# Row-tiled fill in the attention waits of batches 1 and up, v of batch 0 in three head groups, AV moved in the score order

## The chip, the cores and the metric

The kernel runs on one core of one Trainium2 chip. The metric is the device time of one execution in microseconds (us). The engines are TensorE (PE in the profile; its weight loads are PEld), VectorE (DVE), ScalarE (ACT), GpSimd (POOL) and SyncE (SP), which only issues DMAs here.

## The reference

Forgetting attention over 8 batches, 8 heads, 576 positions and a head dimension of 64, and behind it a two-layer network with an exact gelu on 4608 tokens (512 to 2048 to 512).

```python
# attention, for each batch and head
scores = scale * q @ k.T
log_f = np.log(np.clip(f, 0.0001, 1.0))
cum = np.cumsum(log_f, axis=-1)
scores = np.where(causal, -1e9, scores + cum[:, None] - cum[None, :])
attn = softmax(scores)
x = attn @ v                    # heads side by side: 4608 x 512
# feed-forward
h = x @ w_in                    # 512 x 2048
out = gelu_exact(h) @ w_out     # 2048 x 512
```

## The kernel before

**Attention.** Heads are taken in four pairs (`HP`, index `i`), head 0 of a pair on partitions 0 to 63 and head 1 on 64 to 127. For each pair the causal scores are made transposed (keys on partitions) in four score tiles (`STILES`, index `t`), each one or two blocks of keys for both heads. `scores(b, i, t)` (L270) multiplies kT by qT with 64 contraction rows for each head (L289), into one of two buffers of `s_psum`, and ScalarE takes the exp into `e` (L299). Since there are two buffers, the matmuls of a score tile wait until the exp of the tile before the last is done. From pair 1 of batch 1 on, the mask is put on by POOL after the exp (L301). The decay is folded into v: `weigh_v` (L253) multiplies v by exp(-cum) on POOL (or DVE) and adds a column of weights, so that the row sum comes out of the same product. AV is `attend` (L313): 15 matmuls for a head (L320), with e as the weights, into an `o_psum` buffer; `normalize` (L328) divides on DVE (L333, L334). `to_xT` or a DMA transpose turns x for the next product.

**Feed-forward.** For each batch `gemm1` (L370) makes 16 blocks of h from w_in (L375), each in an `m_psum` bank that ScalarE empties by the gelu (L392). The second product, with w_out, is not made at once: it is cut into steps, which are generators (`yield` after a step), and taken as fill between the score tiles of the next batch, where TensorE would wait for ScalarE. `take(fill, n)` takes n steps; the tables `FILL` (batches 3 to 7), `FILL_2` (batch 2) and `FILL_1` (batch 1) give n after each score tile, and their last row the number taken before the AV of pair 3.

**Row-tiled steps.** `gemm2_rows` (L446) makes a 128 x 512 output block in 16 steps from a string: "n" is one matmul with 128 contraction rows into the first bank; "r" is two matmuls of 64 rows each, one on each half of the array, into two banks. At the end DVE copies the second bank to SBUF (L474) and adds the first (L476). `PLAN` gives, for batches 3 to 7, four blocks: which pool holds the two banks ("o", "m", "s") and the string. Batch 0's second product is split in two halves of `n_ff`: `gemm2_half` (L485) uses 128-row steps (L501) for two output blocks, half 0 in the waits of batch 1, half 1 at the head of batch 2's fill (`gemm2_third`), where `PLAN_0` and `PLAN_1` follow.

**PSUM.** There are eight banks: two buffers of two banks in `s_psum`, two of one in `o_psum` (tag "o"), two of one in `m_psum` (tag "m"). A new tile takes a buffer of its pool when its former tile has been read.

**Order.** The schedule is written by hand: every engine does its instructions in the order of the program text. In batches 3 to 7 (`attention`, L621) each pair is score tile 0, fill, tile 1, fill, AV of the pair before, tile 2, fill, tile 3, fill. Batch 0 (`first_attention`, L527) and batch 1 (`second_attention`, L656) have orders of their own. SP's queue issues the loads of v (`load_v`, L114: five DMAs, one for each block of keys, of 256-byte rows), POOL's queue those of q, k, w_in and w_out. `gate` (L562) makes POOL wait for a part of v before it issues w_in; `weigh_v` of later head pairs, the loads of v, w_in, q and k for batch 1 stand behind it on POOL and SP.

Of the kernel before, what the change touches and what calls it, by code (L numbers as in the profile page):

```python
# [52 lines left out]
def kernel(  # L53
# [78 lines left out]
    load_v(0, 0, 4)  # L132
# [261 lines left out]
    def gemm2(c):  # L394
# [38 lines left out]
        (1, "m", 5 * "r" + "n" + 9 * "r" + "n"),  # L433
        (2, "m", 9 * "r" + "n" + 6 * "r"),
# [11 lines left out]
    def gemm2_rows(c, plan):  # L446
# [4 lines left out]
        for ts, held, steps in plan:  # L451
# [10 lines left out]
            for kt, step in enumerate(steps):  # L462
                last = kt == steps.rindex("r")
                for r in range(2 if step == "r" else 1):
# [5 lines left out]
                        start=(kt == 0),  # L470
# [14 lines left out]
    def gemm2_half(c, half):  # L485

        pss = [
            m_psum.tile([P, d_model], FP32, tag="m", name="ps2") for _ in range(2)
        ]
        k0, k1 = half * n_ff // 2, (half + 1) * n_ff // 2  # L490
        if half:
            order = [(ts, kt) for ts in range(2) for kt in range(k0, k1)]
        else:
            order = [
                (ts, kq + kt)
                for kq in (0, 4)
                for ts in range(2)
                for kt in range(4)
            ]
        for ts, kt in order:  # L500
            nc.tensor.matmul(  # L501
                pss[ts],
                g_of[c][kt][:, ts * P : (ts + 1) * P],
                w_out_sb[:, kt, :],
                start=(kt == k0),
                stop=(kt == k1 - 1),
            )
            if kt == k1 - 1 and not half:
                ot_of.append(o_pool.tile([P, d_model], FP32, tag="ot", name="ot"))
                (nc.scalar.copy if ts else nc.vector.tensor_copy)(ot_of[ts], pss[ts])  # L510
            elif kt == k1 - 1:
                nc.vector.tensor_tensor(ot_of[ts], ot_of[ts], pss[ts], Alu.add)
                store(c, ts, ot_of[ts])
            yield
# [12 lines left out]
    def first_attention():  # L527
# [28 lines left out]
        transposes(2, m_psum, "m")  # L556
        scores(0, 1, 1)
# [3 lines left out]
        weigh_v(0, 0, nc.vector)  # L561
        gate = x_pool.tile([P, 1], FP32, tag="gate", name="gate")  # L562
        nc.gpsimd.tensor_copy(gate[D:P], v_sb[D:P, 0, 4, 0:1])
# [11 lines left out]
        load_qk_tokens(1, 4, 8)  # L575
        scores(0, 2, 0)
        scores(0, 2, 1)
        scores(0, 2, 2)
        scores(0, 2, 3)
        attend_head(0, 0)  # L580
        scores(0, 3, 0)
        attend_head(0, 1)
        scores(0, 3, 1)
        attend_head(1, 0)
        scores(0, 3, 2)
        attend_head(1, 1)
        scores(0, 3, 3)
        to_xT(0, 0, nc.vector.tensor_copy)
        attend_head(2, 0)
# [66 lines left out]
    def second_attention():  # L656
# [16 lines left out]
        for i in range(HP):  # L673
            for t in range(4):
# [4 lines left out]
                if i and t in (1, 2):  # L679
                    av(i - 1, t - 1)  # L680
# [81 lines left out]
```

## Time and profile before

| | us |
|---|---|
| median of 8 runs | 349.25 |
| lowest, highest run | 348.09, 350.45 |
| the profiled execution | 349.2 |
| its span, first to last instruction | 347.1 |
| TensorE busy | 331.0 |
| ScalarE busy | 212.6 |
| VectorE busy | 187.6 |
| GpSimd busy | 124.3 |

The granted TensorE clock was 0.998 of full speed. The span falls into batch 0 (until about 40), batch 1 (to 73), batch 2 (to 120), batches 3 to 7 (36.3 each, to 301.5) and the tail with the last products. A line of the timeline is the start, the length of the merged group, engine, line and operation, output and inputs, rows by columns of the TensorE array, shape and type, and the number of instructions; in brackets the idle time of the engine before the group, and what ended it. A line of the chain of waits is start, length, what.

### The profile page before, as it was taken

The numbers are of one execution on the slowest core, as the hardware profiler recorded it, in microseconds if no ns is written. First come the engines' busy times: TensorE is split into PE (matmuls) and PEld (weight loads), VectorE is DVE, ScalarE is ACT, GpSimd is POOL, SyncE is SP. The second block draws the span as 40 slices with busy tenths as digits, with TensorE's granted clock in tenths as the row PEclk, the third lists the DMA queues.
The fourth block names the chain that finished last, engine by engine and source line by source line (L and its number), as shares of the span: only waits on it lengthen the run. The fifth ranks groups of instructions, "written<-read, shape, count | busy, mean of one in ns | idle before, by whom it ended". The sixth has DMA issues, their size and how long they took to land.

```text
span 347.1 us, 7895 instructions
## 1 busy us (share of the span) xinstructions
PE 331.0 (95%) x3182; PEld 175.4 (51%) x3227; DVE 187.6 (54%) x424; ACT 212.6 (61%) x296; POOL 124.3 (36%) x256
## 2 busy tenths in 40 slices
PE   7799999999999999999999999999999999999995
PEld 3574555445554455545654465446544554444443
DVE  5770355943367935796479646975597542021011
ACT  5887786773734787368746973687468765503600
POOL 8390662238318044533445242714270430000000
PEclk9999999999999999999999999999999999999999
DMA  8999999969993999278935995399800130011013
GB/s 119 173 179 195 206 146 169 175 137 160 230 180 94 143 206 178 65 111 163 211 106 75 138 211 136 69 161 205 157 30 2 52 100 30 2 60 60 0 34 90
DMA packets 99924, 43.03 MB, mean 124 GB/s; under 512 B 78704, under 2 KB 95344, under 8 KB 99888
## 3 DMA queue, kind: packets, MB, share of 16 engines
q1 hardware_dynamic: 82592, 28.37, 40.7%
q0 software_dynamic: 16896, 13.63, 26.7%
q8 instruction: 25, 0.41, 0.5%
q10 hardware_dynamic: 400, 0.52, 0.4%
q14 instruction: 11, 0.09, 0.1%
HBM read 36.85 MB, written 9.44 MB: 133 GB/s over the span
## 4 chain that ended last, share of the span: by engine, by line
PE 85%; ACT 6%; issue 3%; POOL 2%; DVE 2%; DMA 2%; POOLq 0%; ACTq 0%; DVEq 0%
PE ps L375 35%; PE ps L466 21%; PE o L320 9%; PE ps L408 8%; PE s L289 7%; ACT e L299 3%; PE ps L501 2%; DMA k<-in_k_dram 2%; ACT L299 2%; PE ps_x L353 1%; ACT g L392 1%; DVE x L334 1%; POOL q L107 1%; PE ps_f L206 1%; POOL k L107 1%
## 5 line engine op out<-in xcount | busy, mean ns | idle before, releaser
L392 ACT ACTIVATE g<-ps 128x512 bf16<-128x512 f32 x144 | 85.3, 597 | 81.1 <-PE ps L375 81.1
L299 ACT ACTIVATE e<-s 128x896 bf16<-128x896 f32 (+2 forms) x128 | 101.5, 836 | 31.9 <-PE s L289 29.2
L375 PE MATMUL ps<-xT,w_in_sb 128*128 128x512 bf16 x497 | 111.4, 379 | 0.8
L466 PE MATMUL ps<-w_out_sb,g 64*128 64x512 bf16 (+1 forms) x731 | 100.5, 376 | 0.8 <-issue 0.8
L375 PEld LDWEIGHTS <-w_in_sb 128*128 128x128 bf16 x576 | 56.0, 98 | 67.5 <-issue 1.8
L301 POOL TENSOR_SCALAR_AFFINE_SELECT e<-e 128x256 bf16<-128x256 bf16 (+1 forms) x135 | 49.3, 383 | 103.3 <-ACT e L299 103.0
L466 PEld LDWEIGHTS <-g 64*128 64x128 bf16 (+1 forms) x756 | 41.5, 94 | 40.9 <-issue 11.9
L289 PE MATMUL s<-qT,kT 64*128 64x320 bf16 (+4 forms) x384 | 45.9, 277 | 4.5 <-ACT e L299 2.7
L244 DVE COPY qT<-tq 64x288 bf16<-64x288 bf16 x96 | 48.7, 507 | 1.4
L260 POOL TENSOR_TENSOR vw<-v_sb,wT 128x640 bf16<-128x640 f32 x31 | 39.7, 1281 | 22.7 <-PE ps L501 12.6
L320 PE MATMUL o<-vw,e 128*128 128x65 bf16 x960 | 36.8, 194 | 3.5 <-issue 2.4
L474 DVE COPY ot<-ps 128x512 f32<-128x512 f32 x26 | 17.9, 690 | 40.3 <-PE ps L466 40.3
L320 PEld LDWEIGHTS <-e 128*128 128x128 bf16 x960 | 34.8, 98 | 5.3 <-PE ps_x L353 0.3
L244 DVE COPY kT<-tk 64x288 bf16<-64x288 bf16 x96 | 32.7, 341 | 1.6
L289 PEld LDWEIGHTS <-kT 64*128 64x128 bf16 x384 | 20.1, 94 | 25.3 <-issue 12.3
L334 DVE TENSOR_TENSOR x<-o,r 128x320 bf16<-128x320 f32 x64 | 31.5, 492 | 2.4 <-DVE r L333 0.2
L417 DVE COPY ot<-ps 128x512 f32<-128x512 f32 (+2 forms) x9 | 5.7, 632 | 48.8 <-PE ps L408 31.9
L408 PE MATMUL ps<-w_out_sb,g 128*128 128x512 bf16 (+2 forms) x142 | 27.9, 355 | 0.1
L333 DVE RECIPROCAL r<-o 128x5 f32<-128x5 f32 x64 | 12.1, 189 | 26.7 <-PE o L320 26.6
L408 PEld LDWEIGHTS <-g 128*128 128x128 bf16 x144 | 13.5, 98 | 14.5
L476 DVE TENSOR_TENSOR ot<-ot,ps 128x512 f32<-128x512 f32 x26 | 17.9, 687 | 1.5
L365 POOL COPY tails<-xT 128x256 bf16<-128x256 bf16 x8 | 3.2, 399 | 31.2 <-DVE xT L356 31.2
(64 smaller groups left out, 158.5 us busy)
## 6 DMA issues: line engine op xcount, KB each, us to landing
out_dram<-ot SPq DMA_DIRECT2D x32, 256.0 KB, 2.3
v_sb<-in_v_dram SPq DMA_DIRECT2D x24, 256.0 KB, 5.2
q<-in_q_dram POOLq DMA_DIRECT2D x6, 576.0 KB, 6.1
k<-in_k_dram POOLq DMA_DIRECT2D x6, 576.0 KB, 8.1
v_sb<-in_v_dram SPq DMA_DIRECT2D x22, 128.0 KB, 5.5
w_in_sb<-in_moe_w_in_dram POOLq DMA_DIRECT2D x4, 512.0 KB, 6.7
w_out_sb<-in_moe_w_out_dram POOLq DMA_DIRECT2D x4, 512.0 KB, 8.3
q<-in_q_dram POOLq DMA_DIRECT2D x4, 144.0 KB, 4.4
```

The costliest lines, as they stand in the source:

```text
L244: nc.vector.tensor_copy(rows[:, odd], src[odd * D : (odd + 1) * D, 2 * i + h].rearrange("d j p -> d p j"),)
L260: eng.tensor_tensor(vw_of[b][:, hs, :, 0:D], v_sb[:, hs, :, :], w.unsqueeze(3).to_broadcast([P, 2, NBLK, D]), Alu.mult,)
L289: nc.tensor.matmul(to, *ab, start=half < 0, stop=half == 1 or not masked)
L299: nc.scalar.activation(et[:, :, z:c], st[:, :, z:c], Act.Exp, scale=scale)
L301: nc.gpsimd.affine_select(out=et[:, :, c0 + z : c0 + P], in_=et[:, :, c0 + z : c0 + P], compare_op=Alu.is_ge, fill=0.0, base=z, pattern=[[ ...
L320: nc.tensor.matmul(o[:, m, :], e_of[b, i, t][:, h, c : c + P], vw_of[b][:, 2 * i + h, n, :], start=(n == 0), stop=(n == m),)
L334: nc.vector.tensor_tensor(x_of[b, i][:, :, h, :], o[:, :, 0:D], r.unsqueeze(2).to_broadcast([P, NBLK, D]), Alu.mult,)
L375: nc.tensor.matmul(ps, w_in_sb[:, kt, ffb * P : (ffb + 1) * P], src[:, kt, 0:TC], start=(kt == 0), stop=(kt == n_dm - 1),)
L392: nc.scalar.activation(g_of[c][ffb], ps, Act.Gelu)
L408: nc.tensor.matmul(pss[ts][:, c0:c1], g_of[c][kt][:, ts * P : (ts + 1) * P], w_out_sb[:, kt, c0:c1], start=(kt == 0), stop=(kt == n_ff - 1),)
L466: nc.tensor.matmul(banks[r], g_of[c][kt][rows, ts * P : (ts + 1) * P], w_out_sb[rows, kt, :], start=(kt == 0), stop=last if r else kt == n ...
L474: nc.vector.tensor_copy(ot, banks[1])
```

## The change

Six edits, all in the order or the form of the work; the arithmetic is the same but for the order of sums.

1. v of batch 0 is loaded in three groups of heads (0-1, 2-3, 4-7) instead of two (0-3, 4-7).
2. The gate waits for a load of the second group (head 2, block 2), over all partitions, instead of the last of the first group.
3. In batch 0, the weighing of v for heads 0 and 1 on DVE moves ahead of the transposes of pair 3, and AV of pair 0 starts before the scores of pair 2, where it stood behind all four of them; the rest follows.
4. `gemm2_half` becomes row-tiled: one output block at a time, two banks, eight steps of two 64-row matmuls, and two DVE operations to empty them; the first block of half 1 uses `o_psum`.
5. In batch 1 the fill starts in pair 1 (`FILL_1`), both AVs of pairs 1 and 2 stand behind tile 1 of the next pair, and one `to_xT` moves.
6. In batches 3 to 7 `FILL` takes one step more behind tiles 0 and 1 of pair 0 (one less behind tile 2), and one step behind tile 0 of the other pairs (one less behind tile 1), seven instead of eight before the AV of pair 3; `PLAN` moves its "n" steps so that each is again the last before an AV, which makes one of them the first step of block 2, and the `start` flag follows.

```diff
--- before.py
+++ after.py
@@ -129,7 +129,8 @@
     make_identity(nc, ident_bf)
     load_qk_tokens(0, 4, 6)
     nc.gpsimd.memset(v_sb[:, :, 0, 0:1], 0.0)
-    load_v(0, 0, 4)
+    load_v(0, 0, 2)
+    load_v(0, 2, 4)
 
 
     key_of = consts.tile([P, 2, P], BF16)
@@ -430,8 +431,8 @@
 
     PLAN = [
         (0, "o", 16 * "r"),
-        (1, "m", 5 * "r" + "n" + 9 * "r" + "n"),
-        (2, "m", 9 * "r" + "n" + 6 * "r"),
+        (1, "m", 6 * "r" + "n" + 9 * "r"),
+        (2, "m", "n" + 9 * "r" + "n" + 5 * "r"),
         (3, "s", 7 * "r" + 9 * "n"),
     ]
 
@@ -467,7 +468,7 @@
                         banks[r],
                         g_of[c][kt][rows, ts * P : (ts + 1) * P],
                         w_out_sb[rows, kt, :],
-                        start=(kt == 0),
+                        start=kt == (steps.index("r") if r else 0),
                         stop=last if r else kt == n_ff - 1,
                     )
                 if kt == n_ff - 1 if held == "s" else last:
@@ -484,34 +485,37 @@
 
     def gemm2_half(c, half):
 
-        pss = [
-            m_psum.tile([P, d_model], FP32, tag="m", name="ps2") for _ in range(2)
-        ]
+
         k0, k1 = half * n_ff // 2, (half + 1) * n_ff // 2
-        if half:
-            order = [(ts, kt) for ts in range(2) for kt in range(k0, k1)]
-        else:
-            order = [
-                (ts, kq + kt)
-                for kq in (0, 4)
-                for ts in range(2)
-                for kt in range(4)
+        for ts in range(2):
+            pool, held = (o_psum, "o") if half and not ts else (m_psum, "m")
+            banks = [
+                pool.tile([P, d_model], FP32, tag=held, name="ps2") for _ in range(2)
             ]
-        for ts, kt in order:
-            nc.tensor.matmul(
-                pss[ts],
-                g_of[c][kt][:, ts * P : (ts + 1) * P],
-                w_out_sb[:, kt, :],
-                start=(kt == k0),
-                stop=(kt == k1 - 1),
-            )
-            if kt == k1 - 1 and not half:
-                ot_of.append(o_pool.tile([P, d_model], FP32, tag="ot", name="ot"))
-                (nc.scalar.copy if ts else nc.vector.tensor_copy)(ot_of[ts], pss[ts])
-            elif kt == k1 - 1:
-                nc.vector.tensor_tensor(ot_of[ts], ot_of[ts], pss[ts], Alu.add)
-                store(c, ts, ot_of[ts])
-            yield
+            for kt in range(k0, k1):
+                for r in range(2):
+                    rows = slice(r * D, (r + 1) * D)
+                    nc.tensor.matmul(
+                        banks[r],
+                        g_of[c][kt][rows, ts * P : (ts + 1) * P],
+                        w_out_sb[rows, kt, :],
+                        start=(kt == k0),
+                        stop=(kt == k1 - 1),
+                    )
+                if kt == k1 - 1:
+                    if not half:
+                        ot_of.append(
+                            o_pool.tile([P, d_model], FP32, tag="ot", name="ot")
+                        )
+                        nc.vector.tensor_copy(ot_of[ts], banks[0])
+                    else:
+                        nc.vector.tensor_tensor(
+                            ot_of[ts], ot_of[ts], banks[0], Alu.add
+                        )
+                    nc.vector.tensor_tensor(ot_of[ts], ot_of[ts], banks[1], Alu.add)
+                    if half:
+                        store(c, ts, ot_of[ts])
+                yield
 
     def gemm2_third():
         yield from gemm2_half(0, 1)
@@ -554,13 +558,13 @@
         nc.vector.tensor_copy(wT[D:P, 4, :], psw[D:P, 4, :])
         scores(0, 1, 0)
         transposes(2, m_psum, "m")
+        weigh_v(0, 0, nc.vector)
         scores(0, 1, 1)
         scores(0, 1, 2)
         transposes(3, m_psum, "m")
         scores(0, 1, 3)
-        weigh_v(0, 0, nc.vector)
         gate = x_pool.tile([P, 1], FP32, tag="gate", name="gate")
-        nc.gpsimd.tensor_copy(gate[D:P], v_sb[D:P, 0, 4, 0:1])
+        nc.gpsimd.tensor_copy(gate, v_sb[:, 2, 2, 0:1])
         load_w_in(0)
         weigh_v(0, 1)
         load_w_in(1)
@@ -573,21 +577,21 @@
         load_w_in(3)
         load_qk_tokens(1, 0, 4)
         load_qk_tokens(1, 4, 8)
+        attend_head(0, 0)
         scores(0, 2, 0)
+        attend_head(0, 1)
         scores(0, 2, 1)
         scores(0, 2, 2)
+        attend_head(1, 0)
         scores(0, 2, 3)
-        attend_head(0, 0)
+        attend_head(1, 1)
         scores(0, 3, 0)
-        attend_head(0, 1)
+        to_xT(0, 0, nc.vector.tensor_copy)
         scores(0, 3, 1)
-        attend_head(1, 0)
+        attend_head(2, 0)
         scores(0, 3, 2)
-        attend_head(1, 1)
+        attend_head(2, 1)
         scores(0, 3, 3)
-        to_xT(0, 0, nc.vector.tensor_copy)
-        attend_head(2, 0)
-        attend_head(2, 1)
         to_xT(0, 1, nc.scalar.copy)
         attend_head(3, 0)
         both = s_psum.tile([P, 2, 1024], BF16, tag="s", name="ps_x2")
@@ -614,9 +618,9 @@
 
 
 
-    FILL = [[6, 5, 4, 3], [0, 4, 3, 3], [0, 4, 3, 3], [0, 4, 3, 3], [8]]
+    FILL = [[7, 6, 3, 3], [1, 3, 3, 3], [1, 3, 3, 3], [1, 3, 3, 3], [7]]
     FILL_2 = [[8, 8, 8, 8], [8, 8, 4, 4], [4, 4, 4, 4], [4, 4, 4, 4], [8]]
-    FILL_1 = [[0, 0, 0, 0], [0, 0, 0, 0], [2, 2, 2, 2], [2, 2, 2, 2]]
+    FILL_1 = [[0, 0, 0, 0], [2, 0, 0, 2], [0, 4, 2, 2], [1, 2, 0, 1]]
 
     def attention(b):
 
@@ -676,10 +680,13 @@
                 if i == 0 and t < 3:
                     transposes(t + 1, *((m_psum, "m") if t == 1 else (o_psum, "o")))
                 take(fill, FILL_1[i][t])
-                if i and t in (1, 2):
-                    av(i - 1, t - 1)
-                if i > 1 and t == 0:
+                if i == 2 and t == 0 or i == 3 and t == 1:
                     to_xT(b, i - 2, nc.vector.tensor_copy, o_psum, "o")
+                if i == 1 and t in (1, 2):
+                    av(0, t - 1)
+                if i > 1 and t == 1:
+                    av(i - 1, 0)
+                    av(i - 1, 1)
                 if (i, t) == (1, 3):
                     load_qk_tokens(2, which="k")
                 if (i, t) == (3, 0):
```

## The prediction

> **What bounds the kernel now.** I read the page's busy times and its chain first, then the timeline of one late batch (the stretch from 228.9 to 265.2 us, which repeats every 36.3 us), then batches 1, 2 and 0.
>
> ```profile
> PE 331.0 (95%) x3182; PEld 175.4 (51%) x3227; DVE 187.6 (54%) x424; ACT 212.6 (61%) x296; POOL 124.3 (36%) x256
> PE 85%; ACT 6%; issue 3%; POOL 2%; DVE 2%; DMA 2%; POOLq 0%; ACTq 0%; DVEq 0%
> ```
>
> TensorE is the bound: 331.0 of 347.1 us, and 85% of the chain. No matmul is removed, so only waits of TensorE and drains between its modes can be gained, about 16 us in all. In the late batch they are these:
>
> ```profile
> 230.56 1.24 PE L466 MATMUL ps<-w_out_sb,g 64*128 64x512 bf16 x10
> 230.92 3.13 ACT L299 ACTIVATE e<-s 128x896 bf16<-128x896 f32 x4
> 231.88 0.37 PE L289 MATMUL s<-qT,kT 64*128 64x448 bf16 x2
> ...
> 237.93 0.74 PE L289 MATMUL s<-qT,kT 64*128 64x256 bf16 x8
> 238.49 0.82 PE L466 MATMUL ps<-w_out_sb,g 64*128 64x512 bf16 x6
> 239.35 0.69 DVE L474 COPY ot<-ps 128x512 f32<-128x512 f32 x1 [2.08 <-PE ps L466]
> 239.47 1.11 PE L320 MATMUL o<-vw,e 128*128 128x65 bf16 x30 [0.16 <-issue]
> 240.15 0.69 DVE L476 TENSOR_TENSOR ot<-ot,ps 128x512 f32<-128x512 f32 x1
> 240.72 0.97 PE L466 MATMUL ps<-w_out_sb,g 64*128 64x512 bf16 x6
> ```
>
> Ends of matmuls are modelled and overlap, so I compare starts. A fill step of two half-row matmuls takes 0.216 us (lower down: 16 of them, 1.73 us in the chain). Ten matmuls from 230.56 are five steps and end at 231.64; the next score tile starts at 231.88, when the first exp (0.92 us from 230.92) is done: 0.24 us of wait. Score tiles 0 and 1 of pair 2 start at 237.93 and their fill at 238.49: 0.56 us where the tiles alone take 0.19 + 0.16, so 0.20 us of wait; the same reading gives 0.18 for pair 1 and about 0.17 for pair 3. The rest of the batch is dense.
>
> **What the skill says.** TensorEngine Tiling (Array Packing), Key Properties: a change of tiling mode drains TensorE. The chain agrees and gives the price:
>
> ```profile
> 73.47 1.83 PE ps L501 x8
> ...
> 77.70 1.73 PE ps L466 x16
> ```
>
> Eight full steps before a row-tiled score tile take 0.10 us more than eight row-tiled ones; the way in costs the same (score tile 73.10, full fill 73.40: 0.30 against 0.19 at 81.12). The same page, Gotcha 1: PSUM Pressure: row tiles write different banks, and evacuation may become the limit. Here each row-tiled output block holds two banks and needs two DVE passes of 0.69 us (L474, L476). TensorE: Matmul & The Clock Gate, Part 3, The mechanism: matmuls are strictly first in, first out. The trace agrees (AV, ready, starts behind the score tile that waits 0.49 us at 45.58), so a fill matmul that waits stops all behind it. DMA: Bandwidth & Descriptors, Anatomy of one DMA: about 2.0 us fixed per transfer, which overlaps; the fastest v load took 2.6 us to land.
>
> **Batches 3 to 7 (FILL, PLAN).** Per batch the gains are: two more steps before tile 2 of pair 0, and one step between tiles 0 and 1 of pairs 1, 2 and 3, with one fewer after tile 1. Going through the batch with the starts above (tile 0 0.19, tile 1 0.16, tile 2 0.20, tile 3 0.14, step 0.216): tile 2 of pair 0 moves from 231.88 to 232.08, tile 1 of pair 1 stays at 234.10 (exp bound), with two more steps done: 0.43 gained. AV of pair 0 starts 0.22 sooner. Tile 1 of pair 2 then starts at 238.11 with the extra step behind it.
>
> Now the step that costs. The steps taken are 7, 13, 16, 19, then 20, 23, 26, 29, then 30, 33: tile 1 of pair 2 takes steps 30, 31 and 32. Steps 30 and 31 end block ts 1, and step 32 is the new leading "n" of block ts 2, whose two banks come from the same two m_psum buffers. It must wait for DVE to empty one. Before, step 32 stood behind AV of pair 1 (1.05 us) and waited little: the six matmuls at 240.72 take 0.97 instead of 0.82, since the first starts (240.72) before the add ends (240.84), the second after it. So the new block's first bank is the one that the copy (L474) releases, the second that of the add. After: the last "r" starts at t, the copy at t + 0.43 (238.92 to 239.35), ends at t + 1.12, and "n" starts at t + 1.17. Unhindered it would start at t + 0.33 (step 0.216, drain 0.11). The stall is 0.84 us, and AV of pair 1, the scores of tiles 2 and 3 and all later exps stand behind it. The old 0.17 at 240.72 goes.
>
> Following on: AV of pair 1 moves from 239.47 to 239.88, tile 1 of pair 3 from 242.68 to 242.96 (exp and TensorE arrive together), AV of pair 2 from 243.82 to 243.89; the last fill before AV of pair 3 has one step fewer, so that AV, and the batch's end, comes 0.15 us sooner. Nothing else there changes its mode switches: every "n" still stands just before an AV. Five batches: -0.75 us.
>
> **Batch 2.** gemm2_half(0, 1) fills two waits with full-row steps: four mode switches of 0.10 to 0.11, all removed: -0.4. Added are two adds of 0.69 on DVE, which here waits for TensorE (3.57 us idle before its first add); the o_psum banks of its first block are empty about 1 us before step 16. The weight loads double, beside the matmuls, as in the other row-tiled fills.
>
> **Batch 1.** TensorE waits for exps:
>
> ```profile
> 45.58 0.34 PE L289 MATMUL s<-qT,kT 64*128 64x64 bf16 x4 [0.49 <-ACT e L299]
> 47.90 0.37 PE L289 MATMUL s<-qT,kT 64*128 64x256 bf16 x4 [0.28 <-ACT e L299]
> 48.20 0.39 PE L501 MATMUL ps<-w_out_sb,g 128*128 128x512 bf16 x1
> ```
>
> Two steps (0.43) fit before 45.58 and two before 47.90, free. Pairs 2 and 3 then have twelve steps instead of sixteen (-0.87) and four mode switches fewer each (about -0.8). But both AVs now stand behind tile 1: in pair 2, tile 1 starts at 48.58 (before 49.02), four steps, a drain and two AVs put tile 2 at 50.75 (before 50.30), and ACT runs dry for about 1.2 us; in pair 3 two steps, to_xT and two AVs put tile 2 at 54.93 (before 54.78). Tile 3's exp ends at 56.90 (before 57.21). The new DVE adds (four passes of 0.69 where there were a copy on DVE and one on ACT) hold the bank of step 8's second row about 0.3 us, and end before xT of pair 2 has to be copied out. So -0.2; bounds -0.9 (AVs hidden better) and +0.5. w_out's first chunk lands at 44.5, and the first fill comes at 44.9 less what batch 0 gains: a tie, in the bounds.
>
> **Batch 0.** The weights and v:
>
> ```profile
> 14.43 0.56 PE L206 MATMUL ps_f<-ident_bf,k 96*64 96x96 bf16 x12 [0.54 <-DMA k<-in_k_dram]
> 16.11 0.20 PE L289 MATMUL s<-qT,kT 64*128 64x64 bf16 x2 [0.43 <-ACT e L299]
> 16.92 0.37 PE L289 MATMUL s<-qT,kT 64*128 64x448 bf16 x2 [0.44 <-ACT e L299]
> 17.62 0.31 PE L289 MATMUL s<-qT,kT 64*128 64x320 bf16 x2 [0.25 <-ACT e L299]
> ```
>
> The wait for k of heads 6 and 7 stays. After it, 1.1 us of waits on exps can hold AV (0.58 a head), if v is weighted by 15.2. Heads 0 and 1 are a quarter of the bytes; the first five v loads land from 10.3 to 15.0, so I put this quarter at 11 to 13, and the weighing on DVE (0.82 us, now ahead of two copies of 0.76) between 13.3 and 14.3. SP issues 15 loads instead of 10 (about 0.5 us each[...]). The gate falls on the eighth load, which may land about 1 us sooner than 14.95, so w_in starts sooner and meets the third v group. POOL's queue behind the gate: w_in, three weighings of 1.3, v of batch 1, q and k; v of heads 4 and 5 is needed at 20.4 instead of 21.9, when it is weighted now by 20.0. Stepping through gives exps ending at 23.1 instead of 22.56, but the AV that follows starts at 23.1 instead of 23.57 (it waited for DVE to free its bank): -0.45. k landing sooner, since less v is queued before it, could give up to 1 us more; a late third group costs up to 0.5. I take -0.7, bounds -1.5 and +0.5.
>
> **Sum.** -0.75 - 0.4 - 0.2 - 0.7 = -2.05 us. The profiled execution took 349.2 (span 347.1), and the median of the runs is 349.25, so the same base serves: 347.2.
>
> **Rivals.**
> *No change* (349.0): batches 0 and 1 give nothing (+0.9), and the stall is 0.2 longer in five batches (+1.0): -0.15 is left. For it: ACT runs dry in batch 1.
> *Slower* (350.9): the leading "n" gets the bank of the add, not of the copy. It then waits 0.74 us more, in five batches +3.7. It decides from a stall of 1.25 us on (0.84 + 2.05/5). Against it: the start at 240.72.
> *Much faster* (343.0): the "n" finds a free bank and doesn't stall: 5 x 0.84 = 4.2 us more. Against it: m_psum has two buffers, and both are held by block ts 1.
>
> **How the numbers follow.** Forecast 0.55 (346.0 to 348.6), no change 0.20, slower 0.17, much faster 0.08. The range 345.2 to 350.0 leaves out the last two in part. This kernel's measurement can't tell less than 0.3% (1.05 us) from nothing: faster is below 348.2. Faster: 0.48 of the forecast and 0.08, 0.56; within: 0.07 and 0.18, 0.25; slower 0.17 and 0.02, 0.19.
>
> **What would show it.** In a late batch: no wait before tile 2 of pair 0, a gap of about 0.8 us before the first AV matmul of pair 1 that ends with L474, a period of 36.15. In batch 2, L501 rows of 64. In batch 1, ACT idle about 1.2 us before tile 2 of pair 2. The prediction is wrong if the gap is absent or 1.5 us, or if batch 0's gemm1 starts later than 25.1.

## The result, and the profile after

| | median, us | lowest to highest | ratio to before |
|---|---|---|---|
| before, 56 runs | 348.93 | 348.05 to 352.75 | |
| changed, 19 runs | 351.92 | 348.70 to 354.29 | 1.006, 95% interval 1.0039 to 1.0081 |

The change makes the kernel 0.6% slower; the forecast was 0.6% faster, and the median lies above its range. The execution profiled with the result is a long one (358.2 us, TensorE clock 0.982, above all 19 runs of the table), so a second profile of the same kernel, called *again* below (353.4 us, span 351.0), stands beside it. In the changed kernel the lines are one higher up to the half product, whose matmul is L498 for L501 (scores L290, AV L321, copy L475).

The page of *again*, busy times and chain by engine:

```profile
PE 330.6 (94%) x3221; PEld 175.4 (50%) x3259; DVE 192.1 (55%) x429; ACT 211.8 (60%) x295; POOL 124.4 (35%) x256
...
PE 81%; DMA 8%; POOL 3%; issue 3%; DVE 2%; SPq 2%; ACT 0%; POOLq 0%; DVEq 0%; ACTq 0%
```

TensorE is as busy as before (331.0), and the span is 3.9 us longer (of the 4.2 us by which this execution is longer than the one profiled before, 0.4 lie outside the span): waits were added, and DMA, 2% of the chain before, is 8% now. Where they lie, the starts of the stages tell (a stage runs to the next one's first matmul; the last stage, the tail, starts with the matmul on the tails of x; worked out from the timelines):

| stage, us | before | again | profile of the result | old v (experiment 3) | edits 1 to 3 alone (experiment 9, second profile) |
|---|---|---|---|---|---|
| batch 0, to its first L376 | 25.10 | 24.29 | 30.29 | 25.08 | 25.64 |
| batch 0, gemm1 | 15.40 | 15.41 | 15.40 | 15.41 | 15.40 |
| batch 1, attention | 18.26 | 22.83 | 18.28 | 18.27 | 18.26 |
| batch 1, gemm1 | 14.34 | 14.35 | 14.34 | 14.34 | 14.34 |
| batch 2, attention | 33.00 | 32.57 | 32.57 | 32.97 | 33.01 |
| batch 2, gemm1 | 13.91 | 14.52 | 17.74 | 13.90 | 13.91 |
| batches 3 to 7 and on, to the tail | 195.20 | 194.52 | 194.55 | 194.53 | 195.21 |
| tail | 31.93 | 32.51 | 32.58 | 31.89 | 32.60 |
| span | 347.14 | 351.00 | 355.75 | 346.39 | 348.37 |

Batches 2 to 7 did what the prediction says (-0.43, and -0.68 in the five late ones). Four rows lose: batch 1 in *again* (+4.57), batch 0 in the profile of the result (+5.19), gemm1 of batch 2 in both (+0.61 and +3.83), and the tail wherever v is loaded in three groups (+0.6).

**Batch 1.** The timeline of TensorE in *again*, leaving out lines between:

```profile
43.91 0.37 PE L290 MATMUL s<-qT,kT 64*128 64x256 bf16 x4
46.24 1.04 PE L498 MATMUL ps<-w_out_sb,g 64*128 64x512 bf16 x4 [1.96 <-DMA w_out_sb<-in_moe_w_out_dram]
47.06 0.53 PE L290 MATMUL s<-qT,kT 64*128 64x64 bf16 x4
...
50.13 1.06 PE L498 MATMUL ps<-w_out_sb,g 64*128 64x512 bf16 x4
```

The first fill step, new behind tile 0 of pair 1, stands for 1.96 us for the first chunk of w_out, issued at 37.9 (before: 37.8) and landed at 46.2 (44.5). Before, its first use was at 48.20. Its four matmuls then last 1.04 where four take 0.60 elsewhere. Windows of *again*, and of before (start and end, length, busy times with counts of PE, PEld, DVE, ACT and POOL, then clock, DMA share and GB/s):

```profile
44.00:46.00 2.00, 0.28 (x4) 0.02 (x3) 0.84 (x2) 1.51 (x2) 0.99 (x4) 0.94 1.13 180
46.00:52.00 6.00, 5.76 (x55) 3.28 (x55) 1.38 (x4) 2.77 (x4) 1.86 (x6) 0.50 0.72 113
```

```profile
44.00:46.00 2.00, 1.51 (x36) 0.96 (x31) 1.64 (x3) 1.84 (x3) 1.37 (x2) 1.00 1.24 209
46.00:52.00 6.00, 5.67 (x87) 3.55 (x86) 2.81 (x9) 5.01 (x7) 3.91 (x10) 1.00 0.86 119
```

From the end of the wait on TensorE has half its clock for 6 us (0.50 against 1.00), and gets through 55 matmuls where it did 87. Old v, experiment 3, has the same batch 1 without the wait: counted from the start of the batch, *again* is 2.1 us behind it at the first fill (46.24) and 4.6 us behind at 54.54, when the clock is full again. So of the 4.57 us 1.96 are the wait, and the remaining 2.6 fall into this stretch.

**Batch 0.** The timeline of POOL and TensorE in the profile of the result:

```profile
14.26 0.79 POOL L170 DMA_DIRECT2D w_in_sb<-in_moe_w_in_dram  x1
...
23.52 1.27 POOL L261 TENSOR_TENSOR vw<-v_sb,wT 128x640 bf16<-128x640 f32 x1 [6.26 <-DMA v_sb<-in_v_dram]
...
25.02 0.98 PE L321 MATMUL o<-vw,e 128*128 128x65 bf16 x15 [5.63 <-POOL vw L267]
```

AV of head 4 stands 5.63 us for v of its head, the new third group (the clock is half for 6.8 us from 22.3 on, within this wait). The last load of that group was issued at 14.83, 0.57 behind w_in's first chunk; its issue in this profile, and the one of *again* (issued at 14.9, w_in 0.4 behind it), with the time to landing at the end of the line:

```profile
v_sb<-in_v_dram SPq DMA_DIRECT2D x1, 64.0 KB, 8.5
```

```profile
v_sb<-in_v_dram SPq DMA_DIRECT2D x1, 64.0 KB, 2.6
```

The -0.81 of *again* in the first row is not a gain of the new order. Four profiles have batch 0 as it was: that of before, that of experiment 2, and the first and the last of experiment 13. There gemm1 starts at 25.10, 24.67, 24.06 and 24.16, by when k of heads 6 and 7 lands (14.38, 13.96, 13.30, 13.67). The first matmul on this k, and gemm1, in the first profile of experiment 13 and in *again*:

```profile
13.42 0.53 PE L206 MATMUL ps_f<-ident_bf,k 96*64 96x96 bf16 x12
...
24.06 0.81 PE L375 MATMUL ps<-xT,w_in_sb 128*128 128x512 bf16 x3
```

```profile
13.51 0.53 PE L207 MATMUL ps_f<-ident_bf,k 96*64 96x96 bf16 x12
...
24.29 0.81 PE L376 MATMUL ps<-xT,w_in_sb 128*128 128x512 bf16 x3
```

From that matmul to gemm1 the four take 10.45 to 10.67 us, and *again* takes 10.78: its batch 0 is shorter than before's since k landed 0.97 us sooner (13.41). Whether three groups of v make k land sooner is not settled (12.85 to 14.37 in 14 profiles, 13.30 to 14.38 in the six with two groups).

**Batches 3 to 7.** The chain of waits in *again*, late batch (start, length, what):

```profile
241.99 0.45 PE ps L467 x4
242.46 0.70 DVE ot L475
243.17 0.04 issue
243.21 0.38 PE ps L467
243.59 0.95 PE o L321 x30
```

The leading n stands for the copy, and AV of pair 1 behind it, as worked out: no fill runs from 242.46 to 243.21. In *again* the timeline gives this wait as 0.78 (predicted 0.84).

### The profile page after: what moved, and what is told of

Same layout as the page of the kernel before. It is cut to its first block, busy times and chain, and to the rows that moved or that the text cites. A ratio compares the mean times of both kernels' runs of the same rounds, so it can differ in the third digit from the quotient of the medians.

```text
span 355.8 us, 7969 instructions
## 1 busy us (share of the span) xinstructions
PE 331.2 (93%) x3221; PEld 175.8 (49%) x3259; DVE 192.2 (54%) x429; ACT 211.4 (59%) x295; POOL 124.2 (35%) x256
## 4 chain that ended last, share of the span: by engine, by line
PE 86%; DMA 3%; issue 3%; DVE 2%; SPq 2%; POOL 2%; ACT 1%; POOLq 0%; ACTq 0%; DVEq 0%
PE ps L376 35%; PE ps L467 24%; PE o L321 9%; PE ps L409 8%; PE s L290 7%; DMA v_sb<-in_v_dram 2%; SPq L119 2%; PE ps L498 2%; PE ps_x L354 1%; DVE ot L475 1%; DMA xT<-x 1%; ACT e L300 1%; POOL q L107 1%; DVE x L335 1%; PE ps_f L207 1%
## 5 line engine op out<-in xcount | busy, mean ns | idle before, releaser
L376 PE MATMUL ps<-xT,w_in_sb 128*128 128x512 bf16 x497 | 113.2, 383 | 2.8 <-DMA xT<-x 2.0
L467 PE MATMUL ps<-w_out_sb,g 64*128 64x512 bf16 (+1 forms) x736 | 104.0, 376 | 4.7 <-DVE ot L475 3.9
L376 PEld LDWEIGHTS <-w_in_sb 128*128 128x128 bf16 x576 | 56.4, 98 | 70.9 <-issue 6.4
L467 PEld LDWEIGHTS <-g 64*128 64x128 bf16 (+1 forms) x756 | 39.9, 94 | 40.5 <-issue 10.6
L245 DVE COPY qT<-tq 64x288 bf16<-64x288 bf16 x96 | 46.8, 487 | 1.4
L321 PE MATMUL o<-vw,e 128*128 128x65 bf16 x960 | 38.0, 196 | 9.0 <-POOL vw L267 5.6
L290 PE MATMUL s<-qT,kT 64*128 64x320 bf16 (+4 forms) x384 | 44.4, 278 | 1.7 <-ACT e L300 0.8
L321 PEld LDWEIGHTS <-e 128*128 128x128 bf16 x960 | 35.5, 99 | 15.2 <-issue 6.6
L475 DVE COPY ot<-ps 128x512 f32<-128x512 f32 x26 | 17.9, 689 | 37.2 <-PE ps L467 37.2
L245 DVE COPY kT<-tk 64x288 bf16<-64x288 bf16 x96 | 36.9, 384 | 1.6
L290 PEld LDWEIGHTS <-kT 64*128 64x128 bf16 x384 | 18.9, 94 | 20.7 <-issue 4.1
```

The source lines that it names most:

```text
L245: nc.vector.tensor_copy(rows[:, odd], src[odd * D : (odd + 1) * D, 2 * i + h].rearrange("d j p -> d p j"),)
L290: nc.tensor.matmul(to, *ab, start=half < 0, stop=half == 1 or not masked)
L321: nc.tensor.matmul(o[:, m, :], e_of[b, i, t][:, h, c : c + P], vw_of[b][:, 2 * i + h, n, :], start=(n == 0), stop=(n == m),)
L376: nc.tensor.matmul(ps, w_in_sb[:, kt, ffb * P : (ffb + 1) * P], src[:, kt, 0:TC], start=(kt == 0), stop=(kt == n_dm - 1),)
L467: nc.tensor.matmul(banks[r], g_of[c][kt][rows, ts * P : (ts + 1) * P], w_out_sb[rows, kt, :], start=kt == (steps.index("r") if r else 0), ...
L475: nc.vector.tensor_copy(ot, banks[1])
```

## Experiments

Expectations of the first eight runs name theories by letters: A, the third group of v comes late since w_in's loads start ahead of it; B, the loss is the leading n's stall; C, a lower clock alone; D, fifteen loads instead of ten are late by SP's issuing; E, batch 1's first fill stands for w_out, and the clock falls behind that. Runs of one group share their runs of before; medians of before were 348.78 (first four), 349.53 (next four), 348.86 and 349.08 (the last two groups of four); the two further profiles in 9 have one run of before, 348.81.

**1. The same kernel again.** No edit.

> The changed kernel once more, for a second profile. Theory A (the third group of v lands late because w_in, released by the earlier gate, runs beside it): the AV of head 4 in batch 0 waits for the weighing of v by 1 to 6 us, varying from run to run, and batch 0's gemm1 starts between 24.5 and 30; time 350 to 353. Theory B (the loss is the leading full-row step of block 2 in batches 3 to 7): that wait is small here and the late batches take over 36.7 us each. Theory C (a lower granted clock or a slow load elsewhere made the profiled run long): no wait over 1 us in batch 0, time near 349.

351.78, ratio 1.0089 (1.0059 to 1.0118). It gave the profile above: the loss repeats, and the clock before the wait in batch 1 is full, so C alone falls. A's wait isn't in this execution: AV of head 4 doesn't wait, AV of head 2 stands 0.73 us for its v. Its six times run from 349.32 to 353.43: waits on DMAs differ from execution to execution.

**2. Tables of batches 3 to 7 alone.**

```diff
# before.py, with the changed PLAN, FILL and start flag only
-    FILL = [[6, 5, 4, 3], [0, 4, 3, 3], [0, 4, 3, 3], [0, 4, 3, 3], [8]]
+    FILL = [[7, 6, 3, 3], [1, 3, 3, 3], [1, 3, 3, 3], [1, 3, 3, 3], [7]]
```

> The kernel before with FILL, PLAN and the start flag of the change alone (batches 3 to 7). My sum gives 0.15 us less in each of five batches: about 348.3, a period of 36.15, with a wait of 0.8 us on L474 ahead of AV of pair 1. Theory B: 352 or more. A bank released by the add would give a wait of 1.5 us and about 352.

348.68, 0.9992 (0.9972 to 1.0011), the period 36.17 instead of 36.29: the small gain, with its stall, is there in the trace, though the time can't be told from before's. B is not the loss.

**3. v in two groups, with the former gate; the rest changed ("old v").**

```diff
-    load_v(0, 0, 2)
-    load_v(0, 2, 4)
+    load_v(0, 0, 4)
...
-        nc.gpsimd.tensor_copy(gate, v_sb[:, 2, 2, 0:1])
+        nc.gpsimd.tensor_copy(gate[D:P], v_sb[D:P, 0, 4, 0:1])
```

> The changed kernel with v in two groups and the gate of the kernel before; order of batch 0 and all fills as changed. Theory A: heads 0 to 3 land near 15.0, so the first AV waits for the weighing until about 16, but no wait over 1 us behind it; gemm1 of batch 0 starts at 24.5 to 25.5, time 347.5 to 349. Theory B: 351 or more.

349.09, 1.001 (0.9997 to 1.0023). This edit alone takes back most of the loss. Batch 0 ends at 25.08: the first AV has to wait for its v, and from the matmul on k it takes 11.2 us; and batch 1 is 18.27: its first fill comes at 44.90, and w_out had landed at 44.77, so it escapes the wait by 0.13 us. A second profile of this very kernel, under the name old_v_no_stall:

> The run with the former loads and gate of v once more, as a look beside the others: the first fill step meets w_out about when it lands (44.8 before), so a wait of 0 to 0.5 us; span 346.4, within 0.5 of it.

350.0, span 347.96: chunk 0 landed at 45.2, the first fill came at 45.4 without a wait. Batch 0 was 0.5 us longer, and AV in batch 2 stood 0.7 us for the mask on POOL: the span expected, 346.4, was missed by 1.6.

**4. The gate behind the last load of the third group.** The weighing of heads 2 and 3 goes ahead of it.

```diff
-        nc.gpsimd.tensor_copy(gate, v_sb[:, 2, 2, 0:1])
+        nc.gpsimd.tensor_copy(gate[D:P], v_sb[D:P, 4, 4, 0:1])
```

> The changed kernel with w_in queued behind the last load of the third group of v (and the weighing of heads 2 and 3 ahead of the gate). Theory A: the third group lands by about 17.5, AV of head 4 waits less than 0.5 us, gemm1 of batch 0 starts near 23.6 instead of 25.1 in the kernel before, and the time is 346 to 348. Theory B: still 351 or more. Theory D (fifteen v loads instead of ten are late by themselves, through SP's issue): AV of head 4 still waits over 2 us, time 350 or more.

353.5, 1.0135 (1.0114 to 1.0157): worse. v lands by 17.6, so D falls, but AV of head 4 still stands:

```profile
21.32 0.63 PE L321 MATMUL o<-vw,e 128*128 128x65 bf16 x15 [1.81 <-POOL vw L267]
```

POOL issues two chunks of w_in from 18.2 on, behind the gate, and weighs v of heads 4 and 5 only then, from 19.8 to 21.3. The clock is half for 3.4 us behind this wait, and batch 0 ends at 26.39. So A's forecast of this run fails as well: v in time is not enough, since the gate also holds the weighing. The first fill of batch 1 stands for w_out here as well. The timeline and the window behind it:

```profile
48.00 0.61 PE L498 MATMUL ps<-w_out_sb,g 64*128 64x512 bf16 x4 [1.62 <-DMA w_out_sb<-in_moe_w_out_dram]
```

```profile
47.00:50.00 3.00, 2.00 (x38) 1.36 (x39) 0.58 (x2) 1.69 (x3) 1.32 (x5) 1.00 1.25 197
```

A wait of 1.62 us, and here the clock stays at 1.00: batch 1's attention is 19.82, only the wait longer. So E's second part isn't tied to every such wait.

**5. The gate on the first group.**

```diff
-        nc.gpsimd.tensor_copy(gate, v_sb[:, 2, 2, 0:1])
+        nc.gpsimd.tensor_copy(gate, v_sb[:, 0, 2, 0:1])
```

> The changed kernel with the gate on a load of the first group of v, so that w_in is issued near 11, ahead of the whole third group. Theory A (a v load issued after w_in lands with it): the last v load lands after 20, AV of head 4 waits 3 to 7 us in every run, time 354 or more. If the late third group in the first profile had another cause: no wait over 1 us there, time near 352 or less.

352.21, 1.01 (1.005 to 1.015). With w_in issued at 11.1, all five loads of the third group land from 18.3 to 21.1, AV of head 4 stands 2.78 us, the clock is half for 3.4 us behind it, and batch 0 ends at 27.84. A's mechanism is there, w_in ahead of v delays v, but the wait and the time are smaller than A expected (3 to 7 us, 354).

**6. w_out ahead of the first weighing of batch 1's v on POOL.**

```diff
                 if ffb == 12:
-                    weigh_v(1, 0)
                     load_w_out(0)
                     load_w_out(1)
+                    weigh_v(1, 0)
```

> The changed kernel with w_out's first two chunks issued ahead of the weighing of v for batch 1 on POOL, so that they don't stand behind v's landing. Theory E: w_out lands before 44, the first fill step of batch 1 doesn't wait, time 347 to 348.5. Theory A: about 351.5. If bandwidth alone sets w_out's landing, it lands near 46 as before and the time stays near 352.

356.98, 1.021 (1.0172 to 1.0248), much worse. No wait for w_out is left in batch 1. Its list of waits begins (sum, times, longest):

```profile
PE o L321 <- POOL e L302: 6.5, 4, 5.0
```

The last three loads of v of batch 1 now land from 45.9 to 50.3 (before: 41.7 to 42.4), POOL waits for them in the weighing, and the masks behind it on POOL hold AV; the clock is half for 6.8 us from 52.1 on, within the longest of these waits. From 10 to 50 us the DMA engines are full or nearly so (shares of 0.8 to 1.3 in stretches of 2 us), and here what was put first delayed the next.

**7. The first fill of batch 1 in pair 2.**

```diff
-    FILL_1 = [[0, 0, 0, 0], [2, 0, 0, 2], [0, 4, 2, 2], [1, 2, 0, 1]]
+    FILL_1 = [[0, 0, 0, 0], [0, 0, 0, 0], [2, 4, 2, 2], [2, 2, 1, 1]]
```

> The changed kernel with batch 1's sixteen fill steps all in pairs 2 and 3, so none needs w_out before about 48. Theory E (the usual loss is the first fill step of batch 1, which waits about 2 us for w_out's first chunk, and the clock that drops after this idle time): no wait on w_out, clock near 1.00 between 46 and 52, and 347.5 to 349 where the changed kernel has 352. Theory A (the third group of v is the usual loss): still about 351.5.

350.49, 1.004 (1.0014 to 1.0066), between what E and A expected. No wait for w_out, but batch 1's attention takes 20.06 us: the second output block follows the first too closely for its banks:

```profile
PE ps L498 <- DVE ot L510: 0.7, 1, 0.7
PE ps L498 <- DVE ot L515: 0.4, 1, 0.4
```

**8. Three edits together** (w_out first, the gate on the third group's first load, and tables without the leading n).

```diff
-        nc.gpsimd.tensor_copy(gate, v_sb[:, 2, 2, 0:1])
+        nc.gpsimd.tensor_copy(gate, v_sb[:, 4, 0, 0:1])
...
-        (2, "m", "n" + 9 * "r" + "n" + 5 * "r"),
+        (2, "m", 10 * "r" + "n" + 5 * "r"),
```

> The changed kernel with w_out first, the gate on the first load of v's third group (weighing of heads 2 and 3 ahead of it), and the full-row step taken from the head of block 2: pair 2's tile 1 takes two steps, the second the last of block 1. My sum: batch 0 -0.8, batch 2 -0.4, and in each of five batches 0.8 less (the stall of 0.84 gone): 343 to 345. If the wait on L474 is only moved, about 347.5.

354.1, 1.0132 (1.009 to 1.0175): batch 1's attention takes 28.85 us, with waits for masks as in experiment 6 and, though w_out is issued at 26.5, one of 2.09 us for its first chunk, which lands only at 47.2; the clock is half for 6.8 us twice. The late batches take 35.49 instead of 36.17, so what the stall costs is 0.68 each.

**9. Edits 1 to 3 alone** on the kernel before, and two further profiles of it.

> Edits 1 to 3 alone on the kernel before; batch 1 and everything behind it is the kernel before's, so the first product with w_out is needed at about 47.4 us instead of 44. Theory 1 (the loss is the meeting of batch 0's new order with the earlier need of w_out): batch 0 ends about 0.8 us sooner and nothing later is lost, 0.997 to 0.999 of before, unless the third group of v is late in an execution. Theory 2 (the new order of the loads loses by itself, since w_in goes ahead of the third group of v in the DMA queues): AV of head 4 waits 1 to 5 us in most executions, first matmul with w_in at 26 to 30 instead of 25.1, 1.003 to 1.012 of before. Theory 3 (the row-tiled work costs clock): no change in the clock here, and 0.998.

> Edits 1 to 3 alone once more, for a profile of another execution: seventeen of its twenty-two times lay above 349.2, up to 353.3, and the one profiled was among the short ones (349.05). If the third group of v is what makes them long, an execution of 350 or more shows AV of head 4 waiting 1 us or more for its v in batch 0, and batches 1 to 7 as before; one of 349 shows it below 0.6. In either, the time from the last copy on DVE to the span's end is 4.0 us, where kernels with v in two groups have 3.4.

> The same kernel as b0_look1, a second execution, with the same expectations: AV of head 4 waits 1 us or more where the execution takes 350 or more, and 4.0 us lie behind the last copy.

350.15, 1.0038 (1.0015 to 1.006). The three profiled executions:

| | last v load lands | AV of head 4 waits | batch 0 ends | tail | time |
|---|---|---|---|---|---|
| first profile | 18.5 | 0.16 | 24.19 | 32.58 | 349.05 |
| second (b0_look1) | 19.9 | 1.22 | 25.64 | 32.60 | 350.2 |
| third (b0_look2) | 19.6 | 0.84 | 25.32 | 32.48 | 349.73 |

Batches 1 to 7 are those of before in the second and third. Counted from the first matmul on k of heads 6 and 7, batch 0 takes 10.26, 11.87 and 10.90 us, against the 10.45 to 10.67 of the former order: edits 1 to 3 gain 0.2 to 0.4 us where v is in time, lose 0.2 to 1.4 where it isn't, and lose 0.6 in the tail in each. The tail, in the chain of before and of edits 1 to 3 (its last piece; the span is in the head line):

```profile
core 0 of [0], span 347.1 us
...
343.45 0.29 DVE ot L417
```

```profile
core 0 of [0], span 347.2 us
...
342.87 0.29 DVE ot L418
```

The last copy ends 0.6 us sooner, and the span not at all. From the copy's end to the span's end it takes 3.40 us in the first and 4.05 in the second; in all 14 profiles with v in three groups 3.95 to 4.09, in all 6 with two groups 3.33 to 3.40. The trace's events show how. In the first, SP's last store is issued 0.03 us after the copy and lands 2.0 later. In the second it first waits until 343.41 for its semaphore, which an earlier store has to signal, is issued 0.33 us after the copy, and lands 2.5 later. So the last landing comes 2.8 us after the copy instead of 2.3, and SP, which then goes through its final semaphores in a fixed order of about 0.06 us each, has five to go instead of three. Five more DMAs at the start have moved the turn in which DMAs get their semaphores. That is a reading of the events, not tested by itself. Nor does the device time follow the span to the last tenth: what lies outside the span is 1.98 to 2.06 us with v in two groups, 1.82 to 1.85 in the four profiles of edits 1 to 3 alone (11 is the fourth), and 2.01 to 2.47 in the other ten; why was not tested.

**10. The first fill of batch 1 behind tile 3 of pair 1.**

```diff
-    FILL_1 = [[0, 0, 0, 0], [2, 0, 0, 2], [0, 4, 2, 2], [1, 2, 0, 1]]
+    FILL_1 = [[0, 0, 0, 0], [0, 0, 0, 2], [2, 4, 2, 2], [1, 2, 0, 1]]
```

> The changed kernel with the first fill of batch 1 moved from behind tile 0 to behind tile 3 of pair 1 (about 3 us later), the same sixteen steps in all. Theory 1 (wait for w_out and the half clock behind it): no wait for w_out, TensorE at full clock, batch 1 from its first scores to its first matmul with w_in 18.0 to 18.6 us where the changed kernel's second profile shows 22.8; time 347 to 348.5, 0.995 to 1.000 of before, if the third group of v is in time, and up to 351 where it isn't. Theory 2 (the third group of v is most of the loss): little is gained, 350.5 to 352, and AV of head 4 waits more than 2 us in batch 0. Theory 3 (the order of the AVs in batch 1 is the loss): batch 1 stays above 20 us.

350.49, 1.003 (1.0012 to 1.0048). The w_out wait is gone and batch 1 is 18.70; but the third group was late in the profiled execution (19.65; it is the longest of the 19 runs), and the clock fell behind it. AV of head 4, and the windows that follow:

```profile
21.32 0.63 PE L321 MATMUL o<-vw,e 128*128 128x65 bf16 x15 [1.59 <-POOL vw L267]
```

```profile
22.00:24.00 2.00, 2.00 (x33) 1.49 (x30) 1.36 (x4) 1.37 (x2) 1.89 (x5) 0.68 0.67 113
24.00:26.00 2.00, 2.00 (x34) 1.96 (x32) 0.69 (x2) 1.27 (x3) 2.00 (x4) 0.50 0.90 112
```

**11. Edits 1 to 3 with w_in behind all loads of v**, on the kernel before.

```diff
+        weigh_v(0, 1)
         gate = x_pool.tile([P, 1], FP32, tag="gate", name="gate")
-        nc.gpsimd.tensor_copy(gate, v_sb[:, 2, 2, 0:1])
+        nc.gpsimd.tensor_copy(gate, v_sb[:, 4, 0, 0:1])
         load_w_in(0)
-        weigh_v(0, 1)
```

> Edits 1 to 3 alone, with the gate on the first load of v's third group and the weighing of head 1 to 2's v ahead of it on GpSimd, so that w_in is issued at 15.5 to 16.5, behind the last load of v (14.9). Theory 1 (v queued behind w_in is what lost in edits 1 to 3 alone): third group landed by 17.6, AV of head 4 waits less than 0.6 us, batch 0 ends at 24.2 to 24.8, 0.996 to 1.000 of before, and fewer long executions. Theory 2 (fifteen small loads instead of ten lose by themselves, or w_in later is as dear): 1.002 or more, and batch 0's end at 25.1 or later.

351.53, 1.005 (1.0023 to 1.0077), no better than 9. In the profiled execution (349.74) the last v load, issued at 14.9, lands at 19.3 although w_in is issued at 16.8, and AV of head 4 stands 1.28 us. Theory 1 of this run falls in its simple form: putting w_in behind v in the order of issue doesn't bring v in time. What holds the load in this execution stays open.

**12. Both mends on the changed kernel** (10 and 11).

> The changed kernel with this gate and the first fill of batch 1 behind tile 3 of pair 1. If both waits together are all of the loss: 346.8 to 347.8, 0.994 to 0.998 of before, the forecast's time. If there is a third loss: 349 or more, 1.000 and above.

351.02, 1.0038 (1.0014 to 1.0061). There is a third loss, as the second branch says, besides the tail; the timeline of batch 1:

```profile
47.65 0.59 PE L498 MATMUL ps<-w_out_sb,g 64*128 64x512 bf16 x4
48.09 0.37 PE L290 MATMUL s<-qT,kT 64*128 64x256 bf16 x4
48.28 0.61 PE L498 MATMUL ps<-w_out_sb,g 64*128 64x512 bf16 x4
...
50.53 1.04 PE L498 MATMUL ps<-w_out_sb,g 64*128 64x512 bf16 x8 [0.98 <-DMA w_out_sb<-in_moe_w_out_dram]
```

The fifth step stands for w_out's *second* chunk. The former half took four steps of both output blocks before it went on to the second chunk, so needed it at the ninth step; the row-tiled one holds two banks for one block, goes through all eight steps of it, and needs the chunk at the fifth. In batch 2 of this execution AV stands another 1.2 us for masks on POOL, which had waited until 79.46 for v of batch 2.

**13. Without the stall.** The tables of 8 on the kernel before; on 12; and on everything changed but batch 0 (loads, gate, order as before) with the fill of 10.

```diff
-        (1, "m", 6 * "r" + "n" + 9 * "r"),
-        (2, "m", "n" + 9 * "r" + "n" + 5 * "r"),
+        (1, "m", 6 * "r" + "n" + 8 * "r" + "n"),
+        (2, "m", 10 * "r" + "n" + 5 * "r"),
...
-    FILL = [[7, 6, 3, 3], [1, 3, 3, 3], [1, 3, 3, 3], [1, 3, 3, 3], [7]]
+    FILL = [[7, 6, 3, 3], [1, 3, 3, 3], [1, 2, 4, 3], [1, 3, 3, 3], [7]]
```

> The kernel before with the tables of batches 3 to 7 alone, and the leading n of block 2 moved behind a third step, so that it stands behind AV of pair 1. If the stall of 0.8 us for the copy is what the changed kernel pays in each of these batches: no wait before AV of pair 1, period 35.5 instead of 36.29, five times 0.8, 344.7 to 345.5, 0.988 to 0.991 of before. If something else takes its place (ScalarE, the add's bank): period 36.0 or more, 347.5 to 348.5.

> The same, with block 2's leading n behind its first ten r steps, so that it stands behind AV of pair 1. Stall gone: five times 0.68 less than two_mends, 3.4 us, 343.5 to 344.5. If the batches 3 to 7 lie behind another limit: within 1 us of two_mends.

> Loads, gate and AV order of batch 0 as in the kernel before, the rest changed, the first fill of batch 1 behind tile 3 of pair 1, and the stall taken away. Sum of parts: before's batch 0, batch 2 -0.4, batches 3 to 7 five times -0.8: 344.3 to 345.0, 0.986 to 0.990, below the run with the tables of batches 3 to 7 alone (0.9902) by about 0.4 us. If the row-tiled half of batch 1 costs in its waits: 345.5 or more.

| | median, us | ratio, 95% interval |
|---|---|---|
| tables alone on the kernel before | 344.93 | 0.9902, 0.9872 to 0.9933 |
| on 12 | 349.16 | 0.997, 0.9944 to 0.9995 |
| all but batch 0 changed | 345.53 | 0.987, 0.9836 to 0.9905 |

The chain of the last one in a late batch shows what the tables do:

```profile
235.94 0.17 PE s L289 x4
236.10 0.54 PE ps L466 x3
236.64 0.95 PE o L320 x30
```

No copy stands in it, the n ends block 1 ahead of AV, and the period is 35.49. The first run is as expected. The second gains 1.9 us on 12 in the median, not the 3.4 expected (both vary by more than 5 us). The third has the lowest ratio of all and beats both kernels, though against the first run the difference lies within the intervals. Its 345.53 is on the branch that the expectation names for a cost of the row-tiled half in batch 1: that stage takes 19.28 us in the profile, where before takes 18.26, with 0.64 us of wait for w_out's second chunk as in 12.

## Why the prediction was wrong, point by point

- **Batches 3 to 7: right.** -0.12 each against -0.15, the stall 0.78 against 0.84, in the place named; there is no wait before tile 2 of pair 0. The rival "slower" gave a time near the measured one by another mechanism, a stall of 1.5, which isn't there.
- **Batch 2: right.** -0.43 against -0.4 (32.57 or 32.58 in seven of the profiles; others lose it again, in part to masks that come late). It said nothing of gemm1 behind it, which stood for a DMA-transposed x in *again* (0.44) and in the profile of the result (1.98, with the clock half for 3.4 us behind it).
- **Batch 0: the gain not shown, the price of its risk wrong.** -0.7 was forecast, and the -0.81 of *again* looks like it. But that is k landing sooner, which the forecast names as an extra; the new order itself, worth 0.45 there, gave at most 0.4 (experiment 9, first profile) and nothing in *again*. That the number fits is luck. The step that failed is "a late third group costs up to 0.5": it saw that w_in starts sooner and meets the third group, but bounded it too low. AV of head 4 stood 0.16, 0.84 and 1.22 us in the three profiles of experiment 9, 1.59 in 10 and 5.63 in the profile of the result, where the last load landed 8.5 us after issue (2.6 to 5.0 in the seven other profiles with this gate). The forecast's own sign of being wrong, gemm1 of batch 0 later than 25.1, was there in four of these five.
- **Batch 1: the step that failed in *again*.** "w_out's first chunk lands at 44.5, and the first fill comes at 44.9 less what batch 0 gains: a tie, in the bounds", and these were -0.9 to +0.5. The 44.5 was one execution's: with the same loads and the same batches 0 and 1, the chunk landed at 45.9 in experiment 2 and at 45.5 in the first run of 13, unseen, since the former fill first uses it at 47.8 and 47.2. In *again* TensorE was ready for it at 44.3 and it landed at 46.2; the price was the wait of 1.96 and the half clock behind it, 4.57 us in all, where the bound was 0.5. The order of the work inside the batch came nearly as worked out (old v, which starts the batch at the same time as before: tile 2 of pair 2 at 50.77 for 50.75, ScalarE dry for 1.08 us, tile 2 of pair 3 at 55.23 for 54.93), but gains 0.0 instead of 0.2 (18.27), and no profile of the changed fill is shorter than before's 18.26. Need of w_out's second chunk at the fifth step (12) was not in it either.
- **The tail: not in the sum.** "SP issues 15 loads instead of 10" was priced by SP's time alone; the 0.6 us that the span has more behind the last copy was nowhere.

So the sum of *again* is -0.81 + 4.57 - 0.43 + 0.61 - 0.68 + 0.58, and with the two gemm1 stages' 0.02 this is the 3.86 by which its span is longer. By ratios: edits 1 to 3 alone 1.0038, the late tables alone 0.9992, all of it 1.006 and 1.009, so in the medians about half of the loss comes with batch 0's loads and order alone (the intervals overlap), and the rest when they meet the other edits: with the former loads and gate all other edits come to 1.001. How a usual execution of 352 us divides its loss is not shown: the two profiles of the changed kernel, of 353.4 and 358.2 us, lose in different places. What lengthens the longest executions (355.5 in 11) was not profiled, and stays open. The forecast's rival "no change" is 349.1 by its own terms, not 349.0; nothing hangs on it.

## What to carry to other kernels

When one stage is made to end sooner, list every load that the next stages first use, with landing and use, and read the landing from several executions: here the same load landed at 44.5, 45.5 and 45.9. A use moves with the compute; a landing need not. A tie between them isn't a bound of half a microsecond: its price is the wait, all that stands behind it in order, and in some executions the clock. Before a shorter stage is put down to an edit, count it from the event that starts it: k's landing alone moved batch 0 by 1 us. And a fill that is made cheaper by taking its blocks one at a time also changes the order in which its weights are needed.

## What the runs showed of the hardware

- The granted clock changes in these profiles only at points that lie a multiple of 3.41 us apart: in *again* it is full for 40.96 us and then half for 6.83, and each half stretch before the tail lasts 3.41 or 6.83 us. Between 8 and 330 us it fell ten times in the twenty profiles, each time behind a stretch of 3.41 us of this grid in which TensorE was busy for 2.00 us or less, and never behind one with 2.05 or more. Here are the stretch before the fall in *again* and the half clock after it, and, from experiment 4, the stretch that holds the wait of 1.62 us:

```profile
42.37:45.78 3.41, 1.88 (x40) 1.25 (x39) 2.47 (x4) 3.00 (x4) 2.40 (x5) 1.00 1.13 174
45.78:52.61 6.83, 6.37 (x61) 3.62 (x63) 1.74 (x5) 3.35 (x4) 2.46 (x6) 0.50 0.71 113
```

```profile
46.64:50.05 3.41, 2.05 (x40) 1.41 (x40) 0.92 (x3) 2.10 (x4) 1.73 (x5) 1.00 1.23 193
```

So waits of 1.96 us (*again*), 1.81 (4, in batch 0) and 1.59 (10) cost the clock, and waits of 1.62 (4, in batch 1), 1.28 (11) and 1.22 (9) did not, by what else lay in their stretch. This is read from the records; no run tested it, and in the tail, stretches with 1.52 to 1.75 us of work kept the clock. The Trainium skill, TensorE: Matmul & The Clock Gate, Part 1: The HAM clock gate, gives a free-running window of about 3.4 us, and a fall after at least one idle window. The grid agrees; but here windows with up to 2.00 us of work were enough, and the measurement decides. Beyond the wait, the half clock cost 2.6 us in *again*; in batch 0 of 4, 5, 10 and the profile of the result, the time from the matmul on k to gemm1, less AV's wait for head 4, is 11.1 to 11.4 us, and 9.8 to 10.7 in 9 and 11, where the clock held.
- The last 64 KB load of v took 2.6 to 5.0 us to land in seven of the eight profiles with the changed gate, and 8.5 in the eighth, where a 512 KB load of w_in had been issued 0.57 us ahead of it on another queue; it took 6.1 with w_in 3.9 us ahead (5). That w_in is all of the cause isn't shown: in 11, with w_in 1.9 us behind, it took 4.4. The same skill's DMA: Bandwidth & Descriptors, Anatomy of one DMA, gives for a DMA that GpSimd issues about 2.0 us fixed and the bytes at 436 GB/s on top, which is, as an estimate from that page, 3.2 us for w_in's first chunk of 512 KB. It took 5.3 to 8.6 us in the twenty profiles, among other loads, and the measurement decides.
- With five more DMAs at the beginning (v in three groups instead of two) the span had 0.6 us more behind the last copy, in 14 profiles against 6 without an overlap.
